# Linear attention and channel mixing on one core: batch 0's loads first on the two hardware queues, weights and batch 1 in a forced order, and a hand-set order for batch 0's attention

## The chip, the cores and the metric

The kernel runs on one core of one Trainium2 chip. The metric is the device time of one execution in microseconds (us). A ratio is the mean time of one kernel's runs over the mean time of the other's runs of the same rounds on the same chip. It is therefore not quite the ratio of the medians that are quoted beside it. The profile comes from one execution, and its span is about 1.8 us shorter than the device time.

## The reference

There are 8 batches of 8 heads, 576 rows and 64 columns. A softmax over the columns of q, a softmax over the rows of k, and two small products give x, which then goes through a channel-mixing block (512 to 1024 to 512).

```python
q_s = softmax(q, axis=-1)              # over 64 columns
k_s = softmax(k, axis=2)               # over 576 rows
kv  = einsum('bhsd,bhse->bhde', k_s, v)
x   = einsum('bhsd,bhde->bhse', q_s, kv)   # -> (8, 576, 512)
x_prev = x shifted down by one row, zeros first
xk = mu_k * x + (1 - mu_k) * x_prev
xr = mu_r * x + (1 - mu_r) * x_prev
out = sigmoid(xr @ w_r) * (maximum(xk @ w_k, 0) ** 2 @ w_v)
```

## The kernel before

The work of a batch comes in two halves of four heads each. A half loads q, k and v (576 KB each, as float32). ScalarE takes exponentials of q and k and casts v. VectorE normalises q. TensorE forms `kvp`, transposes q into `qtp`, and forms `xp`. ScalarE copies `qt` and `xb` out, and VectorE mixes neighbouring rows into `xk` and `xr`. The channel mixing then runs in units of 512, 384 and 256 rows per pair of batches. It projects `xk` with `wk_bf` (`kfp`), takes relu on ScalarE (`rel`) and the square on VectorE (`k2`), and then does two more products (`rp`, `vp`). The attention of later batches is interleaved with the units. In these traces an engine that waits for data starts no later instruction of its own (ScalarE stands for 4.03 us below while the relus behind it have their data).

```python
ldpool = ctx.enter_context(tc.tile_pool(name="ldpool", bufs=3))
...
for m, src in enumerate((moe_mu_k, moe_mu_r)):       # four small transfers, first on ScalarE's queue
    for g in range(2):
        ...
        nc.scalar.dma_start(out=mu_sb[...], in_=ap)
emit_load(0, 0, (nc.sync, nc.scalar, nc.sync))       # q, k, v of the first half
first = emit_load(0, 1, (nc.scalar, nc.sync, nc.scalar))[0]
...
def emit_weights(gate):     # wk and wr in four transfers each of whole rows, wv in two,
    ...                     # all on GpSimd's queue, all gated on `first` (q of the second half)

def unit(pair, c0, n):
    for fc in range(FT):
        kfp = psum.tile([128, 512], F32, tag="mm", bufs=4, name="kfp")
        for ct in range(CT):                         # ct 0, 1: first half; ct 2, 3: second half
            nc.tensor.matmul(kfp[:, 0:n], lhsT=wk_bf[:, ct, fc * 128:(fc + 1) * 128],
                             rhs=xk[:, ct, c0:c0 + n], start=(ct == 0), stop=(ct == CT - 1))
        rel = mpool.tile([128, 512], BF16, tag="rel", bufs=3, name="rel")
        nc.scalar.activation(out=rel[:, 0:n], in_=kfp[:, 0:n], func=ACT.Relu, scale=HALF_ROOT)
        nc.vector.tensor_tensor(out=k2[:, fc, 0:n], in0=rel[:, 0:n], in1=rel[:, 0:n], op=ALU.mult)
        yield n
    ...

emit_weights(first)
a0 = attention(0, 0); next(a0)
a1 = attention(0, 1); next(a1)
emit_mu()                                            # transpose mu on TensorE, copy on VectorE
emit_load(1, 0, (nc.gpsimd,) * 3)                    # batch 1
emit_load(1, 1, (nc.gpsimd,) * 3)
```

The order of these statements is not the order on the engines. A scheduler reorders instructions of the program by its own estimate of when they will be ready, except on engines where the kernel asks for its own order.

The softmax here doesn't subtract the row's maximum and nothing guards it: scores larger than these inputs give would overflow.

## Time and profile before

The median of three runs was 223.57 us (223.4 to 224.09).

| | before |
|---|---|
| TensorE busy, share of the span | 191.7 us, 86% |
| TensorE idle before 33 us | 33 − 12.00 = 21.0 us |
| ScalarE busy from 33 to 58 us | 25.00 of 25 us |
| first kv product starts | 13.75 us |
| first projection on the second half's xk | 29.55 us |
| first relu | 31.95 us |

The page's first part gives each engine's busy time, its share of the span, and the number of instructions.

```profile
span 221.9 us, 3634 instructions
PE 191.7 (86%) x1313; PEld 101.5 (46%) x1313; DVE 166.2 (75%) x367; ACT 147.7 (67%) x229; POOL 37.3 (17%) x58
```

The windows view of the kernel before comes next. Its columns are the window and its length, then the busy us (and instructions) of PE, PEld, DVE, ACT and POOL, then the granted clock of TensorE, the share of the DMA engines, and GB/s.

```profile
0.00:33.00 33.00, 12.00 (x81) 6.72 (x81) 18.08 (x43) 15.57 (x17) 13.57 (x25) 1.00 0.95 258
33.00:48.00 15.00, 13.80 (x107) 7.10 (x107) 13.70 (x30) 15.00 (x21) 5.66 (x8) 1.00 1.02 381
48.00:58.00 10.00, 9.00 (x63) 4.74 (x63) 9.78 (x20) 10.00 (x15) 4.94 (x8) 1.00 1.03 402
```

The first row shows the head: 21 us of TensorE's idle time lie there. ScalarE is busy for every microsecond from 33 to 58 us, while TensorE loses 1.2 us and then 1.0 us.

The timeline of the kernel before follows, with start, length, engine, line, operation, and in brackets the idle time before and what ended it.

```profile
4.95 1.28 ACT L155 ACT_TABLE_LOAD   x1 [4.95 <-DMA raw<-in_q_dram]
11.49 1.16 ACT L155 ACTIVATE eqk<-raw 128x1152 bf16<-128x1152 f32 x1 [4.08 <-DMA raw<-in_k_dram]
13.26 2.40 POOL L118 DMA_DIRECT2D wk_bf<-in_moe_w_k_dram  x4 [10.96 <-DMA raw<-in_q_dram]
13.75 1.16 PE L175 MATMUL kvp<-vv_100,eqk 64*128 64x129 bf16 x18 [7.12 <-ACT vv_100 L159]
...
29.55 1.89 PE L223 MATMUL kfp<-xk,wk_bf 128*128 128x512 bf16 x8 [1.91 <-DVE xk L212]
30.88 1.16 ACT L155 ACTIVATE eqk<-raw 128x1152 bf16<-128x1152 f32 x1 [4.03 <-DMA raw<-in_k_dram]
31.95 0.58 ACT L227 ACTIVATE rel<-kfp 128x512 bf16<-128x512 f32 x1
```

The first half's k lands at 11.4 us and holds up ScalarE. The weights are issued only at 13.26 us. ScalarE then stands 4.03 us in front of k of batch 1, and the relus come behind it, in order, although projection sums already exist. The chain of the work that ended last says the same:

```profile
2.67 10.29 DMA raw<-in_q_dram
14.45 5.93 DMA wk_bf<-in_moe_w_k_dram
20.66 10.20 DMA raw<-in_k_dram
30.88 1.16 ACT eqk L155
```

Up to 31 us, the kernel before is one chain of transfers: the gate for the weights, the weights, then batch 1.

### The profile page before, as it was taken

What the parts mean: (1) busy time and instruction counts of PE and PEld (TensorE: products, weight loads), DVE (VectorE), ACT (ScalarE), POOL (GpSimd) and SP (SyncE); (2) the same over time, 40 slices, a digit from 0 to 9 for tenths busy, and PEclk for the clock granted to TensorE, in tenths of its full rate; (3) what the DMA queues carried; (4) which work ended last, traced back from release to release, by engine and by line L of the source; (5) the groups of instructions that cost most, each with busy time, mean ns of one, the idle gap of its engine ahead of it and who ended that gap; (6) DMA issues with size and microseconds to landing.
All of it is one profiled execution on the core that took longest, in us unless ns stands there. A gap on an engine that the chain in (4) does not pass through costs nothing.

```text
span 221.9 us, 3634 instructions
## 1 busy us (share of the span) xinstructions
PE 191.7 (86%) x1313; PEld 101.5 (46%) x1313; DVE 166.2 (75%) x367; ACT 147.7 (67%) x229; POOL 37.3 (17%) x58
## 2 busy tenths in 40 slices
PE   0045748999999999999999999999999999999990
PEld 0033214444547554445547454446465544454640
DVE  1539758999999898889798998888777757482431
ACT  1396449999976969685939697849736392653440
POOL 2066713253330030330030300000000000000000
PEclk9999999999999999999999999999999999999999
DMA  6979999999999274789075290242131401330413
GB/s 231 385 196 163 205 373 391 390 368 402 414 361 340 108 245 168 228 276 319 14 239 222 42 360 16 50 96 47 35 88 24 95 3 30 76 83 21 108 29 83
DMA packets 15691, 40.61 MB, mean 183 GB/s; under 512 B 2105, under 2 KB 3641, under 8 KB 15673
## 3 DMA queue, kind: packets, MB, share of 16 engines
q0 software_dynamic: 8256, 27.40, 38.4%
q1 hardware_dynamic: 6576, 11.21, 17.2%
q10 hardware_dynamic: 840, 1.77, 2.1%
q8 instruction: 10, 0.16, 0.3%
q14 instruction: 9, 0.07, 0.1%
HBM read 33.56 MB, written 9.44 MB: 194 GB/s over the span
## 4 chain that ended last, share of the span: by engine, by line
PE 57%; DVE 15%; DMA 12%; ACT 10%; issue 2%; ACTq 1%; POOL 1%; DVEq 0%
PE vp L242 23%; PE kfp L223 15%; PE rp L235 11%; DMA raw<-in_q_dram 5%; DMA raw<-in_k_dram 5%; PE xp L195 3%; ACT rel L227 3%; ACT eqk L155 3%; ACT qt L190 3%; DMA wk_bf<-in_moe_w_k_dram 3%; PE kvp L175 3%; DVE rsum L163 2%; DVE xk L212 2%; DVE xm L210 2%; PE qtp L189 2%
## 5 line engine op out<-in xcount | busy, mean ns | idle before, releaser
L223 PE MATMUL kfp<-xk,wk_bf 128*128 128x384 bf16 (+2 forms) x384 | 71.1, 329 | 4.0 <-DVE xk L212 2.3
L227 ACT ACTIVATE rel<-kfp 128x512 bf16<-128x512 f32 (+2 forms) x96 | 45.8, 517 | 20.7 <-PE kfp L223 19.4
L223 PEld LDWEIGHTS <-wk_bf 128*128 128x128 bf16 x384 | 35.8, 98 | 28.8 <-issue 6.8
L155 ACT ACTIVATE eqk<-raw 128x1152 bf16<-128x1152 f32 x32 | 37.9, 1200 | 12.1 <-DMA raw<-in_k_dram 8.1
L245 DVE SCALAR_TENSOR_TENSOR ot<-th,vp 128x512 f32<-128x512 f32 x36 | 24.6, 683 | 17.5 <-PE vp L242 12.7
L238 ACT ACTIVATE th<-rp 128x512 f32<-128x512 f32 x36 | 22.9, 635 | 21.9 <-PE rp L235 20.9
L235 PE MATMUL rp<-wr_bf,xr 128*128 128x512 bf16 x144 | 37.0, 379 | 0.0
L163 DVE TENSOR_REDUCE rsum<-eqk 128x18 f32<-128x1152 bf16 x16 | 21.6, 1349 | 6.5 <-ACT eqk L155 6.4
L74 POOL DMA_DIRECT2D raw<-in_q_dram x14 | 10.2, 731 | 73.2 <-ACT vv_108 L159 31.8
L167 DVE TENSOR_TENSOR qs<-eqk,rrec 128x1152 bf16<-128x1152 bf16 x16 | 21.7, 1356 | 0.8
L210 DVE TENSOR_SCALAR xm<-xd,mu 128x576 bf16<-128x576 bf16 x64 | 21.4, 377 | 0.4
L190 ACT COPY qt<-qtp 128x1152 bf16<-128x1152 bf16 x16 | 18.2, 1137 | 4.3 <-PE qtp L189 4.1
L235 PEld LDWEIGHTS <-xr 128*128 128x128 bf16 x144 | 13.2, 98 | 13.9
L195 PE MATMUL xp<-qt,w 128*128 128x512 bf16 x64 | 13.8, 303 | 5.9 <-ACT qt L190 5.6
L175 PEld LDWEIGHTS <-eqk 64*128 64x128 bf16 x288 | 9.6, 100 | 14.4 <-issue 8.2
L195 PEld LDWEIGHTS <-w 128*128 128x128 bf16 x64 | 6.3, 101 | 14.1 <-issue 7.2
L189 PE MATMUL qtp<-ident,qs 128*128 128x128 bf16 x144 | 11.6, 231 | 0.0
L189 PEld LDWEIGHTS <-qs 128*128 128x128 bf16 x144 | 9.9, 103 | 2.6 <-issue 0.4
L175 PE MATMUL kvp<-vv_100,eqk 64*128 64x129 bf16 x108 | 4.7, 233 | 7.3 <-ACT vv_100 L159 7.3
L74 POOL DMA_DIRECT2D raw<-in_v_dram x14 | 10.1, 723 | 2.3 <-DMA wv_bf<-in_moe_w_v_dram 1.8
L74 POOL DMA_DIRECT2D raw<-in_k_dram x14 | 10.1, 721 | 2.3 <-DMA wv_bf<-in_moe_w_v_dram 1.4
L182 DVE SCALAR_TENSOR_TENSOR w<-kvp,rz,mask 128x128 bf16<-128x128 f32 x32 | 9.7, 339 | 0.4
(81 smaller groups left out, 234.4 us busy)
## 6 DMA issues: line engine op xcount, KB each, us to landing
out_dram<-ot SPq DMA_DIRECT2D x72, 128.0 KB, 2.4
raw<-in_q_dram POOLq DMA_DIRECT2D x14, 576.0 KB, 7.1
raw<-in_k_dram POOLq DMA_DIRECT2D x14, 576.0 KB, 8.0
raw<-in_v_dram POOLq DMA_DIRECT2D x14, 576.0 KB, 9.2
wk_bf<-in_moe_w_k_dram POOLq DMA_DIRECT2D x4, 256.0 KB, 5.4
wv_bf<-in_moe_w_v_dram POOLq DMA_DIRECT2D x2, 512.0 KB, 9.7
raw<-in_q_dram SPq DMA_DIRECT2D x1, 576.0 KB, 3.8
raw<-in_v_dram SPq DMA_DIRECT2D x1, 576.0 KB, 4.8
```

Source lines behind the costliest of these rows:

```text
L74: ld.append(queues[i].dma_start(out=t[:, i, :, :], in_=ap))
L155: nc.scalar.activation(out=eqk[:, i, :, :, :], in_=t[:, i, :, :].rearrange("p u (j d) -> p j u d", d=D), func=ACT.Exp)
L163: nc.vector.reduce_sum(out=rsum[:], in_=eq, axis=AX.X)
L189: nc.tensor.transpose(out=qtp[:, j, :], in_=qs[:, j, :], identity=ident[:])
L190: nc.scalar.copy(out=qt[:], in_=qtp[:, 0:J, :])
L195: nc.tensor.matmul(xp[:, 64 * c:64 * e], lhsT=w[:, hf, :], rhs=qt[:, c:e, 64 * hf:64 * hf + 64], start=True, stop=True)
L210: nc.vector.tensor_scalar(out=xm[:, hf, :], in0=xd[:, hf, :], scalar1=mu[:, c:c + 1], scalar2=None, op0=ALU.mult)
L223: nc.tensor.matmul(kfp[:, 0:n], lhsT=wk_bf[:, ct, fc * 128:(fc + 1) * 128], rhs=xk[:, ct, c0:c0 + n], start=(ct == 0), stop=(ct == CT - 1))
L227: nc.scalar.activation(out=rel[:, 0:n], in_=kfp[:, 0:n], func=ACT.Relu, scale=HALF_ROOT)
L235: nc.tensor.matmul(rp[:], lhsT=xr[:, ct, c0 + 128 * m:c0 + 128 * m + 128], rhs=wr_bf[:, ct, :], start=(ct == 0), stop=(ct == CT - 1))
L242: nc.tensor.matmul(vp[:], lhsT=k2[:, ft, 128 * m:128 * m + 128], rhs=wv_bf[:, ft, :], start=(ft == 0), stop=(ft == FT - 1))
L245: nc.vector.scalar_tensor_tensor(out=ot[:], in0=th[:], scalar=1.0, in1=vp[:], op0=ALU.add, op1=ALU.mult)
```

## The change

The intent was to shorten the head. Batch 0 is to arrive on two hardware queues with q and k first. The weights start as soon as batch 0's first half is in. Batch 1 follows in a forced order, and batch 0's attention runs in an order set by hand on TensorE, VectorE and ScalarE. The diff, cut to its core:

```diff
-    ldpool = ctx.enter_context(tc.tile_pool(name="ldpool", bufs=3))
+    ldpool = ctx.enter_context(tc.tile_pool(name="ldpool", bufs=4))
+    ctx.enter_context(tc.manual_schedule(engines={mybir.EngineType.Pool}))
     (a half is now heads 0,1,4,5 or 2,3,6,7 instead of four neighbours)
+    first = emit_load(0, 0, (nc.sync, nc.scalar, nc.sync))
     for m, src in enumerate((moe_mu_k, moe_mu_r)):
-        for g in range(2):
-            nc.scalar.dma_start(out=mu_sb[...], in_=ap)
-    emit_load(0, 0, (nc.sync, nc.scalar, nc.sync))
-    first = emit_load(0, 1, (nc.scalar, nc.sync, nc.scalar))[0]
+        nc.sync.dma_start(out=mu_sb[4 * m:4 * m + 4, :]..., in_=ap)
+    emit_load(0, 1, (nc.scalar, nc.sync, nc.scalar))
+    warm = const.tile([1, 1], F32, name="warm")
+    nc.vector.memset(warm[:], 0.0)
+    nc.scalar.activation(out=warm[:], in_=warm[:], func=ACT.Exp)
...
+        for h in range(2):                      # wk in column halves: 2 KB runs of the source
+            for u in range(2):
+                ld = part(wk_bf, moe_w_k, F, u, 512 * h, 512 * h + 512)
+                (the first one gated on v of the first half)
+        for u in range(2):
+            part(wr_bf, moe_w_r, C, u, 0, C)
...
-    def unit(pair: int, c0: int, n: int):
+    def unit(pair: int, c0: int, n: int, step: int = 1):
     (with step 4: four kfp tiles get ct 0, 1 first, and then all four get ct 2, 3)
...
+    emit_weights(first[2]); emit_load(1, 0); emit_load(1, 1)
+    with tc.manual_schedule(engines={PE, DVE, Activation}):
+        emit_mu()
+        a0 = Attention(0, 0); a1 = Attention(0, 1)
+        a0.exp(0); a0.exp(1); a0.norm_q(); a0.cast_v(nc.scalar.copy); a1.exp(0)
+        a0.kv("mm"); a0.transpose_q(); a0.copy_qt(); a0.weights()
+        a1.exp(1); a1.norm_q(); a0.x(0); a0.x(1); a1.cast_v(nc.scalar.copy)
+        a1.kv("mm"); a1.transpose_q(); a1.copy_qt(); a0.diff(); a0.mix(0)
+        a1.weights(); a1.x(0); a1.x(1); a1.diff(); a1.mix(0); a0.mix(1); a1.mix(1)
...
-            for c in unit(pair, c0, n):
+            for c in unit(pair, c0, n, 4 if pair == 0 and c0 == 0 else 1):
```

## The prediction

> **What bounds it now.** The page puts TensorE at 191.7 us busy of a 221.9 us span. The windows view places its idle time: 21 us before 33 us, only some 4 us between 33 and 208 us, and about 5 us at the tail. The body is bound by TensorE; only the head can give.
>
> **Head, from the timeline and the waits.** q of the first half batch lands at 4.95 us; ScalarE then loads its table (1.28 us, exposed). k of that half lands only at 11.4 us, behind four mu transfers on its queue and beside batch 1's q (issued at 1.47 us). The v cast, and with it the first kv product, waits to 13.7 us. The weights wait for the second half's q (13.26 us). Batch 1's q is handled in the middle of batch 0's chain (1.2 us ScalarE, 3.0 us VectorE). The second half's xk releases the projection at 29.55 us; ScalarE, in order, stands 4.03 us in front of batch 1's k (lands 30.88 us) before the first relu at 31.95 us.
>
> **What changes, with my estimate.** Rates come from the page: 385 GB/s once running; weights move about 5.2 MB of f32 in some 15 us.
> - Batch 0 alone on two queues: q and k at about 5.2 us, v about 8.3 us, the second half about 12 us. First kv product about 9.5 us instead of 13.7.
> - Table load hidden: 1.3 us on ScalarE, not on the final chain.
> - Against it: the mu transpose and copy now come first in the forced order, and mu is queued behind q and v, so the first row sum may wait until 8.5 us (1.4 us lost).
> - Summing measured durations along the hand-set order (exp 1.16, cast 1.14, qt 1.1, row sum plus reciprocal plus multiply 3.0, w 0.8, mix 1.5 us), the second half's xk is ready at about 24 to 25.6 us, 4 to 5.5 us sooner.
> - Weights, gated on v, start at about 8.5 us and leave no gap in the transfers. All engines share the transfers (the Trainium skill, "DMA: Bandwidth & Descriptors", section "Issuing engines are not separate DMA queues"), so bytes decide: batch 1 then comes whole at about 35 us, only 1 to 3 us sooner than before, its q later than before. This caps the gain: either ScalarE again stands before batch 1's exponentials ahead of relus, or TensorE idles 2 to 3 us before the second unit.
> - TensorE work, tail and steady state: unchanged. The interleaved start exists already (eight first matmuls ran before 29.55 us).
>
> **Result.** The head gives 4 to 6 us if the relus run ahead of batch 1, 1 to 3 us if not; I hold the first the likelier. Predicted 218.3 us, 80% range 214.5 to 221.8. Chances: faster by over 2% 0.58, within 2% 0.38, slower by over 2% 0.04.
>
> **Right or wrong in the profile after.** TensorE busy 190 to 192 us. First kv product near 9.5 to 10 us. Weight issues begin near 8.5 us. First projection matmuls on channels 2 and 3 at 24 to 26 us. Second unit's (128x384) steady matmuls at 47 to 52 us instead of 54.8. TensorE idle before 33 us falls by about 5 us; later it rises by at most 3.
>
> **What would make it wrong.** ScalarE or VectorE, ordered ahead of the data, stalled by batch 1's load; wk column halves (2 KB runs instead of 4 KB) moving slower; two queues not giving k by 6 us; VectorE, nearly full from 33 to 80 us, unable to give batch 1 earlier, so the head's gain returns as idle TensorE.

## The result, and the profile after

The kernel after took 221.38 us in the median of four runs (220.91 to 221.84). The kernel before took 223.66 us in the same rounds (223.4 to 224.09). The ratio is 0.9896 (0.9869 to 0.9922), a gain of 1.0% where I had forecast 2.4%. Executions over 1.5% slower than the fastest of the same kernel are left out of the means.

```profile
span 219.7 us, 3641 instructions
PE 193.5 (88%) x1313; PEld 101.6 (46%) x1313; DVE 166.3 (76%) x384; ACT 147.7 (67%) x230; POOL 35.8 (16%) x56
```

The same windows of the kernel after:

```profile
0.00:33.00 33.00, 14.96 (x88) 7.89 (x89) 17.34 (x45) 16.57 (x21) 13.86 (x25) 0.95 1.03 272
33.00:48.00 15.00, 14.15 (x112) 7.13 (x110) 14.88 (x34) 15.00 (x22) 5.68 (x9) 1.00 1.03 394
48.00:58.00 10.00, 8.98 (x74) 4.83 (x73) 9.99 (x21) 10.00 (x15) 3.67 (x6) 1.00 1.04 406
```

TensorE did 3.0 us more of busy time before 33 us, though with a clock that read 0.95 on average. ScalarE did only 1.0 us more before 33 us, and again it is full from 33 to 58 us.

The timeline of the kernel after, with the lines that answer to those shown of before:

```profile
5.97 2.22 ACT L154 ACTIVATE eqk<-raw 128x1152 bf16<-128x1152 f32 x2 [2.17 <-DMA raw<-in_q_dram]
9.36 1.15 ACT L160 CAST vv_103<-raw 128x1152 bf16<-128x1152 f32 x1 [1.17 <-DMA raw<-in_v_dram]
9.64 2.62 POOL L113 DMA_DIRECT2D wk_bf<-in_moe_w_k_dram  x4 [8.33 <-DMA raw<-in_v_dram]
10.16 1.34 DVE L166 TENSOR_REDUCE rsum<-eqk 128x18 f32<-128x1152 bf16 x1
10.56 1.16 PE L184 MATMUL kvp<-vv_103,eqk 64*128 64x129 bf16 x18 [0.53 <-ACT vv_103 L160]
...
27.82 6.73 PE L270 MATMUL kfp<-xk,wk_bf 128*128 128x512 bf16 x23 [2.92 <-DVE xk L232]
28.95 1.16 ACT L154 ACTIVATE eqk<-raw 128x1152 bf16<-128x1152 f32 x1 [3.68 <-DMA raw<-in_q_dram]
30.02 1.07 ACT L276 ACTIVATE rel<-kfp 128x512 bf16<-128x512 f32 x2
```

The first kv product came 3.2 us sooner (10.56 instead of 13.75 us), and the weights 3.6 us sooner (9.64 instead of 13.26 us). The projection on the second half's xk came only 1.7 us sooner (27.82 instead of 29.55 us) and the first relu 1.9 us. ScalarE still stands in front of batch 1, now in front of its q, for 3.68 us.

The chain of the kernel after, at its start and where it turns:

```profile
2.20 7.45 DMA mu_sb<-in_moe_mu_r_dram
...
21.01 2.56 PE kfp L270 x6
...
27.82 6.73 PE kfp L270 x23
...
36.04 0.64 ACT rel L276
36.67 1.01 ACT qt L207
37.68 0.50 ACT rel L276
38.18 0.49 ACT th L287
```

It starts with a transfer of 2 KB of mu, holds six projection matmuls that stand ahead of the second half's xp products, then 23 matmuls in 6.73 us. From 36.04 to 58.01 us nearly every piece of it is ScalarE. In the kernel before, most of the chain in the same stretch is VectorE, for example:

```profile
36.13 1.36 DVE rsum L163
38.06 1.27 DVE qs L167
41.88 0.75 DVE xk L212
44.17 1.26 DVE rsum L163
```

Summed from 33 to 58 us, ScalarE has 5.0 us of the chain before and 21.8 us after, and VectorE 15.3 and 0 us. Both engines are nearly full there, so the chain runs over one or the other by small differences: in bufs3, below, whose time is nearly that of the kernel after, it is 10.1 and 9.5 us.

As a measure of progress I compare the ends of the VectorE instructions that write the output tiles (36 in each kernel, in order). After minus before is −2.50 us at tile 1, −2.08 at tile 4, −1.88 at tile 8 (which ends at 77.99 us before), and −1.53 at tile 10 (91.95 us). It then stays between −1.53 and −1.70 us to the last tile. (Between tiles 1 and 10 the difference jumps, to −1.16 at tile 2 and −2.53 at tile 5, so single tiles say little.) Everything but the tail was therefore decided before about 92 us. A further 0.6 us of the spans' difference of 2.2 us comes after the last tile.

### The profile page after: what moved, and what is told of

Same layout as the page of the kernel before. It is cut to its first block, busy times and chain, and to the rows that moved or that the text cites. A ratio compares the mean times of both kernels' runs of the same rounds, so it can differ in the third digit from the quotient of the medians.

```text
span 219.7 us, 3641 instructions
## 1 busy us (share of the span) xinstructions
PE 193.5 (88%) x1313; PEld 101.6 (46%) x1313; DVE 166.3 (76%) x384; ACT 147.7 (67%) x230; POOL 35.8 (16%) x56
## 2 busy tenths in 40 slices
DMA packets 16171, 40.62 MB, mean 185 GB/s; under 512 B 2072, under 2 KB 4632, under 8 KB 16152
## 4 chain that ended last, share of the span: by engine, by line
PE 60%; ACT 19%; DVE 13%; DMA 3%; issue 2%; SPq 1%; DVEq 0%; ACTq 0%
PE vp L291 22%; PE kfp L270 19%; PE rp L284 11%; ACT eqk L154 5%; ACT qt L207 4%; ACT rel L276 4%; DMA mu_sb<-in_moe_mu_r_dram 3%; PE kvp L184 3%; PE qtp L202 3%; PE xp L212 2%; DVE rsum L166 2%; DVE xk L232 2%; DVE qs L170 2%; ACT xb_105 L215 2%; ACT xb_109 L215 1%
## 5 line engine op out<-in xcount | busy, mean ns | idle before, releaser
L270 PE MATMUL kfp<-xk,wk_bf 128*128 128x384 bf16 (+2 forms) x384 | 72.6, 335 | 4.3 <-DVE xk L232 3.7
L270 PEld LDWEIGHTS <-wk_bf 128*128 128x128 bf16 x384 | 36.3, 99 | 30.3 <-issue 8.5
```

## The experiments

Eighteen kernels ran. Each ratio is against the kernel before in the same rounds. Some of the expectations name engines by the short names that the profile uses (PE is TensorE, DVE VectorE, ACT ScalarE, POOL GpSimd).

### Which part of the change gave the gain?

**loads_only** keeps the loads, queues and GpSimd order of the kernel after, but leaves batch 0's attention to the scheduler as before:

```diff
-    with tc.manual_schedule(engines={PE, DVE, Activation}):
-        ... the hand-set order ...
+    a0 = attention(0, 0); next(a0)
+    a1 = attention(0, 1); next(a1)
+    emit_mu()
+    for gen in (a0, a1): drain(gen)
-            for c in unit(pair, c0, n, 4 if pair == 0 and c0 == 0 else 1):
+            for c in unit(pair, c0, n):
```

> The changed kernel's loads (queues, weight pieces, gate on v, four raw buffers, forced GpSimd order, early table load), but batch 0's attention emitted as before, in the scheduler's own order, and no interleaved start. If the loads make the gain (theory A: batch 1's arrival and the full ScalarE and VectorE after it set the pace): about 221.4 us, as the change. If the hand-set order makes it (theory H: the chain of batch 0 sets the pace): about 223.5 us. If both give part: 222 to 223 us.

**order_only** is the reverse: the loads, weights and three buffers of the kernel before, with the hand-set order and step 4.

> The kernel before's loads, queues, weight pieces and three raw buffers, with the hand-set order of batch 0's attention and the interleaved start. Theory H: about 221.5 to 222 us. Theory A: 223 to 224 us, as before, since batch 1 arrives as before.

Loads_only took 221.27 us, ratio 0.9877 (0.9854 to 0.9899), which is no worse than the whole change. Order_only took 224.67 us, ratio 1.0036 (1.001 to 1.0063), so a little slower than before. The gain came from the loads; the hand-set order added nothing that these runs show. In order_only the second half's xk was ready 0.4 us sooner than before (29.06 us), but ScalarE took k and v of batch 1 first, at 30.90 and 32.41 us, and the first relu came at 33.46 us, 1.5 us later than before.

**mu_moved** is the kernel before with one edit: the four mu transfers go to the other hardware queue, behind the first half's loads.

```diff
+    emit_load(0, 0, (nc.sync, nc.scalar, nc.sync))
     ...
-            nc.scalar.dma_start(out=mu_sb[...], in_=ap)
+            nc.sync.dma_start(out=mu_sb[...], in_=ap)
-    emit_load(0, 0, (nc.sync, nc.scalar, nc.sync))
```

> The kernel before with one thing changed: the four mu transfers go out on SyncE's queue behind the first half batch's loads, so that the first half's k is first on ScalarE's queue. (The scheduler then also puts batch 1's q behind the weights by itself, as in pool_forced, which alone was 0.6% slower.) If the queue place of k is what delays batch 0 in the kernel before: k lands by 7 us instead of 11.4, the first kv product starts at about 10.5 us, the weights are gated earlier too, and the time is about that of loads_only, 221 to 222 us (ratio 0.986 to 0.993). If the gain needs the other load edits (gate on v, wk pieces, four buffers): 223 to 225 us.

It took 222.4 us, ratio 0.9938 (0.9906 to 0.9969), which is about six tenths of the whole change's gain by the middle values. The exponentials of q and k began at 5.76 us and the first kv product at 10.89 us, nearly as in the kernel after. Its six runs fall into two groups (220.99 to 221.79 and 223.0 to 223.27 us), which I can't explain. The scheduler also moved batch 1's q behind the weights in this kernel, so the edit is not as pure as its diff; pool_forced, next, has that move alone.

**pool_forced** is the kernel before with only the forced GpSimd order added.

> The kernel before with one line more: the GpSimd order is the program's order, so that batch 1's q no longer goes out at 1.5 us but after the weights. Nothing else of the change. If the head start of batch 1's q is what delays batch 0 before (k lands at 11.4 us), about half or more of the change's gain comes from this line: 221.5 to 222.5 us, first kv product at 11 to 12 us. If the other load edits matter (queues, mu off ScalarE's queue, gate on v), 223 to 223.6 us.

It took 225.27 us, ratio 1.0063 (1.0026 to 1.01). The second half's xk was ready at 28.59 us, 0.9 us sooner than before (29.50 us), and yet the kernel was slower. Its first kv product came at 12.71 us, 1.0 us sooner than before, where mu_moved had it 2.9 us sooner; so batch 1's early q was only a part of what delayed batch 0, and the place of mu on the queue the larger part. ScalarE waited 4.86 us for batch 1's q, took it at 30.66 us and its k at 32.16 us, and the first relu came at 33.23 us. **bufs3**, the kernel after with three load buffers, tested the fourth buffer.

> The changed kernel with three raw buffers instead of four; the order on ScalarE is the same. If the fourth buffer has a part in the gain (it lets batch 2's first half be fetched before batch 1's v is cast): 222 to 223 us. If not: 221 to 221.6 us.

It took 221.59 us, ratio 0.9915 (0.9896 to 0.9935), against 0.9896 for the kernel after. The intervals overlap, so the fourth buffer has no part that these runs can show.

### Was it the half clock of TensorE?

The windows of one microsecond show the granted clock of the kernel after at the start of its first unit:

```profile
27.00:28.00 1.00, 0.18 (x1) 0.10 (x1) 0.99 (x3) 0.00 (x0) 0.31 (x1) 0.84 1.00 407
28.00:29.00 1.00, 1.00 (x3) 0.29 (x2) 0.96 (x3) 0.05 (x1) 0.40 (x1) 0.50 1.06 424
31.00:32.00 1.00, 1.00 (x5) 0.39 (x4) 1.00 (x3) 1.00 (x2) 0.68 (x1) 0.95 1.01 383
```

The clock fell to 0.50 after 2.92 us of idle TensorE and stayed there for 3.4 us (from 27.68 to 31.10 us in the trace's clock record). Before, TensorE idled 1.91 us at the same place, and the clock read 1.00. The Trainium skill, "TensorE: Matmul & The Clock Gate", section "What's actually happening", describes such a thing: half the clock after an idle window of some 3.4 us, full clock again after as much activity, with windows that run free of the kernel. The trace agrees on the window's length, but the window before the fall (24.27 to 27.68 us) was not idle throughout: TensorE was busy for 0.63 us of it. Over nineteen traces, each of the 28 recorded windows of 3.41 us at full clock in which TensorE was busy for 0.395 of the time or less is followed by the half clock, and none of the 1041 with 0.422 or more is. The kernel before just escaped, with 0.44 in the window from 26.83 us. (The clock column also reads 1.00 where a trace holds no clock record yet. In the kernel before the record begins at 26.83 us, and 18 kv matmuls take 1.16 us at 13.75 us, against 0.70 us at 33.62 us.) So here was a rival explanation for the missing gain. **filler** adds ten matmuls on data of the first half, into a scratch tile, between the two channel halves of the first group, to keep TensorE busy:

```diff
+                if step > 1 and f0 == 0 and cts[0] == 2:
+                    idle = psum.tile([128, 1024], F32, tag="att", bufs=2, name="idle")
+                    for _ in range(10):
+                        nc.tensor.matmul(idle[:, 0:512], lhsT=wk_bf[:, 0, 0:128],
+                                         rhs=xk[:, 0, c0:c0 + n], start=True, stop=True)
```

> The changed kernel with ten extra matmuls of 512 columns into a scratch tile, put on TensorE between the two halves of the first projection group, where the change has TensorE idle for 2.92 us and its granted clock then falls to 0.50 from 27.8 to 31.0 us. Theory C (the idle gap costs the clock, and the slow matmuls cost time): no half clock after the gap, the 23 projection matmuls take about 5 us instead of 6.73, and the time falls by 1 to 1.5 us, to about 220 us (ratio 0.982 to 0.985). Rival: the clock falls too but ScalarE, which has batch 1's q exponential and the relus in order, sets the pace, and the time stays at 221.4 us (ratio 0.989).

It took 221.65 us, ratio 0.9883 (0.9852 to 0.9914). The clock stayed at 1.00, as it was meant to. Its timeline, in the lines of the first unit, shows what the clock was worth:

```profile
27.94 1.89 PE L275 MATMUL kfp<-xk,wk_bf 128*128 128x512 bf16 x8 [0.72 <-DVE xk L232]
29.49 1.16 ACT L154 ACTIVATE eqk<-raw 128x1152 bf16<-128x1152 f32 x1 [4.35 <-DMA raw<-in_q_dram]
...
31.19 3.70 PE L275 MATMUL kfp<-xk,wk_bf 128*128 128x512 bf16 x15 [1.36 <-ACT rel L281]
```

Eight matmuls took 1.89 us at full clock, and then TensorE waited 1.36 us for a relu. The half clock was real, and its removal gained nothing here, where TensorE then stood waiting for relus. Theory C falls for this kernel. (The profile caught filler's slowest execution, 222.56 us.)

That the half clock costs nothing in general is not shown. The record has the mean granted clock of every execution, and in kernels with a faster head, which come next, a lower clock and a longer time go together. Mu_kfp took 220.0 to 221.18 us in its four executions at 0.996 or more, and 221.81 and 221.91 us in the two at 0.992. Mu_kfp_rel4 took 220.4 and 220.54 us at 1.0, and 221.08 to 222.03 us in its three other fast ones at 0.988 and 0.989. That is about 1 us, but only an association, since idle TensorE time also lowers the clock. Loads_only shows none.

### The head made as short as I had predicted it

Two things had made the head of the kernel after later than my sum. The row sum stood behind the mu copy, which waited for mu until 9.8 us. And six half-speed projection matmuls, from 21.0 to 23.6 us, stood ahead of the second half's xp products. **mu_pool** sends mu on GpSimd's queue, first of all:

```diff
-        nc.sync.dma_start(out=mu_sb[4 * m:4 * m + 4, :]..., in_=ap)
+        nc.gpsimd.dma_start(out=mu_sb[4 * m:4 * m + 4, :]..., in_=ap)
```

> The changed kernel with the two mu transfers on the GpSimd queue at the very start. The first row sum then starts at about 7.2 us instead of 10.16 us, and the second half's xk is ready 1 to 1.6 us before the 27.8 us of the change. Theory H: the time falls by as much, to about 220 us (ratio to before 0.983). Theory A: the time stays at 221 to 221.5 us (ratio 0.988 to 0.991), because ScalarE still waits for batch 1's q and is full from then on.

**kfp_after_x** puts the first projection group after the second half's xp products in the forced order:

```diff
         a1.x(1)
+        u0 = unit(0, 0, 512, 4)
+        early = [next(u0) for _ in range(1)]
```

> The changed kernel with the first projection group held behind the second half's x products on TensorE (in the change six half-clock projection matmuls, 2.6 us, stand between them and the qt copy, which is done at 22.2 us while the x products start at 23.36). Theory H: x products about 1.1 us sooner, second half's xk ready at about 26.7 us; and since the eight projection matmuls now fill the gap before it, no half clock at 27 to 31 us either; together 1.5 to 2.5 us faster than the change, 219 to 220 us. If ScalarE's wait for batch 1's q (28.9 us) sets the pace: no more than 0.5 us faster.

**mu_kfp** does both.

> Both: mu on the GpSimd queue at the start, and the first projection group behind the second half's x products. Theory H: the gains add up, second half's xk at about 25.2 us, and the time 2.5 to 3.5 us below the change, 218 to 219 us, which is what was predicted for the change. If batch 1's arrival sets the pace: no better than the better of the two alone.

| | xk of the second half ready | first relus | time, median | ratio |
|---|---|---|---|---|
| after (own rounds) | 27.8 | 30.02 | 221.38 | 0.9896 (0.9869 to 0.9922) |
| mu_pool | 26.3 | 27.41, 29.31, 30.84 | 220.78 | 0.9863 (0.9833 to 0.9893) |
| kfp_after_x | 27.1 | 29.80 | 223.56 | 0.9974 (0.994 to 1.0008) |
| mu_kfp | 25.1 | 26.17, 29.59 | 220.84 | 0.9863 (0.9828 to 0.9898) |

The first row sum of mu_pool began at 8.18 us, near the 8.5 us of my prediction. In mu_kfp the second half's xk was ready at 25.1 us, inside the 24 to 25.6 us that I had predicted for the change. Yet the time fell by only about half a microsecond against the kernel after, with intervals that overlap. The timeline of mu_kfp shows where those 2.6 us went:

```profile
26.17 0.60 ACT L277 ACTIVATE rel<-kfp 128x512 bf16<-128x512 f32 x1 [3.64 <-PE kfp L271]
28.52 1.16 ACT L155 ACTIVATE eqk<-raw 128x1152 bf16<-128x1152 f32 x1 [1.75 <-DMA raw<-in_q_dram]
29.59 0.58 ACT L277 ACTIVATE rel<-kfp 128x512 bf16<-128x512 f32 x1
30.22 1.02 PE L271 MATMUL kfp<-xk,wk_bf 128*128 128x512 bf16 x4 [1.93 <-ACT rel L277]
```

One relu ran early. Behind it ScalarE, in order, waited 1.75 us for batch 1's q, and the second relu came after that exponential at 29.59 us. TensorE, with its four buffers full, idled 1.93 us. Kfp_after_x had xk sooner than the kernel after and was still slower by its ratio. Its profile caught its fastest run (222.22 us at a clock of 0.998; the five others, at 0.985 to 0.992, took 223.36 to 224.42 us), so I don't explain the ratio from that trace. The clock is a likely part of it.

**mu_filler** put the filler into mu_pool, in case the clock mattered once mu was early. It took 221.93 us, ratio 0.9929 (0.9906 to 0.9952), so no help and rather a loss. But its trace still shows the half clock, from 32.63 to 36.04 us, so the filler did not do what it was for and the question stays unanswered.

> mu_pool with the ten extra matmuls of filler: xk at about 26.3 us, no half clock after the idle gap. If the half clock costs time once the relus run (in mu_pool one relu is ahead of batch 1's q): 219.5 to 220.2 us, 0.5 to 1 us under mu_pool. If not: 220.5 to 221 us.

### Relus first, and batch 1 sooner

If ScalarE's order is the obstacle, relus should go ahead of batch 1. **mu_kfp_rel4** is mu_kfp with four relus forced ahead of batch 1's exponentials:

```diff
+        u0 = unit(0, 0, 512, 4)
+        early = [next(u0) for _ in range(4)]
+        next(att)               # batch 1's first exponentials, after the four relus
```

> The kernel mu_kfp with ScalarE's order forced: the first four relus of the first unit before batch 1's first exponentials (in all kernels so far at least one relu stands behind the exponential of batch 1's q, whose data lands at 28.2 to 29.5 us, so a faster head could not be used). Theory S (ScalarE, in order, stands before batch 1's data with relus behind it): the faster head of mu_kfp (xk at 25.1 us) now counts; fourth relu over by about 28.5 us instead of 33.1, TensorE no longer idle at 29 to 30 us, and the time 2 to 4 us under the change, 217.5 to 219.5 us (ratio 0.971 to 0.980). Rival B (the arrival of the whole of batch 1 and the full ScalarE and VectorE after 33 us set the pace whatever the relus do): about as mu_kfp, 220.5 to 221 us.

It took 221.52 us, ratio 0.9872 (0.9843 to 0.9902). Forcing the relus ahead gained nothing alone.

**b1_before_wv** brings the other side forward: batch 1's first half is loaded before wv.

> The changed kernel with batch 1's first half loaded ahead of wv. Batch 1's q lands about 5 us sooner than the 28.9 us of the change (2.1 MB less ahead of it at about 0.39 MB per us). Theory A: 2 to 4 us faster than the change, 218 to 219.5 us. Theory H: no difference, 221 to 221.5 us, or slower if wv now comes late.

It took 222.9 us, ratio 0.9954 (0.9925 to 0.9983), which is slower than the kernel after. Batch 1's exponentials now ran at 25.05 us, in the middle of batch 0's chain. Its row sum on VectorE began at 26.79 us, ahead of the last xk (28.05 us), which was ready at 28.8 us.

**light_dma** does not load the second half of wv and uses the first half twice, so its result is wrong. It only tests what batch 1 would be worth with 1 MB less ahead of it.

```diff
-        for h in range(2):
+        for h in range(1):
-                                 rhs=wv_bf[:, ft, :], ...
+                                 rhs=wv_bf[:, ft % (FT // 2), :], ...
```

> Wrong result on purpose: the changed kernel without the transfer of the second half of wv (1.05 MB of f32 read), its matmuls reading the first half twice; the same work on every engine. Batch 1's transfers then land about 2.7 us sooner (q at about 26.3 us, v of the second half at about 35.3 instead of 38.0). If batch 1's arrival sets the pace, in the form S or B: 1.5 to 2.7 us faster than the change, 218.7 to 220 us. If the head's own chain does: 221.4 us.

**rel4_light_dma** joins it with mu_kfp_rel4, and is wrong too.

> Wrong result on purpose: mu_kfp_rel4 without the second half of wv. If S alone holds, this is about as mu_kfp_rel4 (the relus no longer stand behind batch 1). If batch 1's arrival still counts after the relus are freed (B): another 1 to 2.5 us faster than mu_kfp_rel4.

Light_dma took 221.17 us, ratio 0.9873 (0.9848 to 0.9897), with batch 1's q used at 26.12 us instead of 28.95. Rel4_light_dma took 219.65 us, ratio 0.9804 (0.9784 to 0.9825). Batch 1 sooner alone moved little, relus and head alone moved little, and both together moved 1.7 to 1.9 us by the medians. This fits two limits that end at nearly the same time, each hiding what the other is worth. The clock is a rival that these runs do not separate: against the two executions of mu_kfp_rel4 at full clock (220.4 and 220.54 us) the step to rel4_light_dma, which ran at 0.994 to 1.0, is only 0.8 us.

The correct form of the pair is **rel4_b1**: mu_kfp_rel4, with batch 1's first half loaded before wv.

> A correct kernel that loosens both waits at once: mu_kfp_rel4 (faster head, four relus ahead of batch 1's exponentials) with batch 1's first half loaded ahead of wv, so that ScalarE's exponentials at about 28 us find their data (q lands at 23.7, v at 26.6 us instead of 31.9). Theory P (head and batch 1's arrival bind in parallel: each loosened alone gave nothing, light_dma 221.2 and mu_kfp_rel4 221.5 us, both together 219.65 us): 219 to 220.3 us. If only the whole of batch 1 (its last v, 38 us) counts: 221 to 222 us, as mu_kfp_rel4.

It took 220.15 us, ratio 0.9844 (0.982 to 0.9868).

### The column halves of wk

**wk_full** is the kernel after with wk in two transfers of whole 4 KB rows instead of four with 2 KB runs.

```diff
-        for h in range(2):
-            for u in range(2):
-                ld = part(wk_bf, moe_w_k, F, u, 512 * h, 512 * h + 512)
+        for u in range(2):
+            ld = part(wk_bf, moe_w_k, F, u, 0, F)
```

> The changed kernel with wk in two transfers of whole rows (4 KB runs of f32, as in the kernel before) instead of four column halves (2 KB runs); ScalarE's order is the same. In the change the weights start 3.6 us sooner than before, yet batch 1's last v lands 1.2 us later (38.0 against 36.8 us). If the short runs make wk slow: batch 1's q lands 0.7 to 1.5 us sooner than 28.95 us, and the time falls by 0.5 to 1.2 us. If not: q lands within 0.4 us of 28.95 us and the time stays at 221.4 us.

It took 220.68 us, ratio 0.9863 (0.984 to 0.9885). The page counts 4632 packets under 2 KB in the kernel after, 3641 before and 3576 here. ScalarE's first exponential of batch 1 began at 28.02 us; in the kernel after it was 28.95 us:

```profile
28.02 1.16 ACT L153 ACTIVATE eqk<-raw 128x1152 bf16<-128x1152 f32 x1 [3.88 <-DMA raw<-in_q_dram]
```

That is 0.93 us sooner at equal bytes, although the first weight issue was 0.16 us later (9.80 us). The tiles from the tenth on came 2.49 us before those of the kernel before, instead of 1.53. The size is not certain, because the landing varies: in five other kernels with the kernel after's loads ScalarE began on batch 1's q at 28.73 to 29.49 us, and in mu_pool at 28.24 us. The wk transfer itself is the better measure. From its first issue to its last landing it took 9.02 us here and 8.45 us in rel4_b1_wk, and 9.40 to 10.59 us in the thirteen kernels with column halves whose profile is in the fast state. So whole rows are faster, and their worth in time, about 0.7 us, is only likely, since the ratios' intervals overlap.

**rel4_b1_wk** puts whole rows into rel4_b1. It is correct.

> The best correct kernel so far (rel4_b1, 220.15 us) with wk in whole rows. If the short runs are slow: about 0.5 to 1 us under rel4_b1, 219.2 to 219.7 us. If not: 220 to 220.3 us.

It took 219.5 us (219.34 to 219.54 in five runs), ratio 0.9805 (0.9786 to 0.9823). This is the best correct kernel, 1.95% under the kernel before. Its windows:

```profile
0.00:33.00 33.00, 16.06 (x117) 8.87 (x118) 20.21 (x50) 19.06 (x24) 14.65 (x26) 1.00 1.03 289
33.00:48.00 15.00, 14.18 (x98) 7.08 (x96) 14.67 (x32) 15.00 (x20) 6.39 (x9) 1.00 1.03 395
48.00:58.00 10.00, 9.29 (x72) 4.94 (x71) 9.97 (x25) 9.96 (x17) 3.61 (x6) 1.00 1.04 407
```

ScalarE did 19.06 us of work before 33 us, against 16.57 in the kernel after and 15.57 before.

### Is VectorE the pace of the first units?

VectorE is nearly full as well from 33 us on (14.88 of 15 us in the kernel after). **light_dve** takes the row sums of batches 1 and 2 over 16 of the 64 columns; its result is wrong.

```diff
-            nc.vector.reduce_sum(out=rsum[:], in_=eq, axis=AX.X)
+            nc.vector.reduce_sum(out=rsum[:], axis=AX.X,
+                                 in_=eq[:, :, 0:16] if self.b in (1, 2) else eq)
```

> Wrong result on purpose: the changed kernel with the row sums of batches 1 and 2 over 16 of 64 columns, so that VectorE has about 4 us less work between 29 and 60 us, where it is 99% busy; orders elsewhere hardly changed. If VectorE's full stretch sets the pace: 1.5 to 4 us faster, 217.5 to 220 us. If arrival and ScalarE's order do: within 0.7 us of the change.

It took 221.09 us, ratio 0.9866 (0.9845 to 0.9888), against 0.9896 for the kernel after. VectorE fell to 13.60 us between 33 and 48 us, ScalarE was still busy 14.95 of 15 us there, and the time hardly moved. So VectorE's load is worth about 0.3 us by the medians, and the intervals overlap. By chance the clock also read 1.00 throughout in the head of the profiled execution (220.98 us), and the executions at 0.989 to 0.991 took 220.84 to 221.23 us, which agrees with filler that the half clock is worth little in this order.

## Why the prediction was wrong, point by point

The time itself, 221.38 us, lies just inside the predicted range (214.5 to 221.8 us), but the gain was less than half of the forecast.

**"The head gives 4 to 6 us if the relus run ahead of batch 1 ... I hold the first the likelier."** This is the step that failed, in three terms.

1. *The second half's xk at 24 to 25.6 us.* It came at 27.8 us. v landed at 9.36 instead of 8.3 us. The mu wait that I had put at 8.5 us lasted until 9.8 us, with the row sum at 10.16 us; mu_pool took this away and won 1.5 us of xk. The six projection matmuls ahead of the xp products were not in my sum; with them moved as well, mu_kfp reached 25.1 us. So this term of the sum was mis-sized by 2.2 us at least, and its two causes are shown.
2. *"Batch 1 then comes whole at about 35 us, only 1 to 3 us sooner."* It came 1.2 us later than before: its last load landed at 38.0 us (issued at 22.81 us, 15.2 us on the way), against 36.8 us before. The bytes did decide, as the Trainium skill, "DMA: Bandwidth & Descriptors", section "Issuing engines are not separate DMA queues", let me assume: all queues share the same engines. But I took the rate for unchanged. The column halves of wk delayed batch 1 by about 1 us (q by 0.93 us and the last load from 36.99 to 38.0 us against wk_full), a risk that I had named and not costed. That makes up the loss against before, but not the 1 to 3 us that I had expected to win; those stay unexplained. (These are single executions; in five other kernels with the same loads the last load landed at 37.15 to 38.53 us.) Before, moreover, one load of batch 1 (its q, issued at 1.47 us) had been moved ahead of the weights, and after the change all of batch 1 stands behind them.
3. *The relus ahead of batch 1.* They did not run ahead. ScalarE waited 3.68 us for batch 1's q and the relus came behind it, which is the branch for which I had written 1 to 3 us. The wait ended 1.9 us sooner than before (28.95 instead of 30.88 us), and the first relu came 1.9 us sooner. The measured gain, 2.3 us, lies in this branch, but in part by luck: I had based 1 to 3 us on batch 1 coming whole that much sooner, and it came later. The second unit's steady matmuls, for which I had said 47 to 52 us, started at 53.54 us (before: 54.76).

The condition in that step was not enough either. Mu_kfp_rel4 forces the relus ahead of batch 1 on the head of mu_kfp, and still took 221.52 us (220.4 and 220.54 us at full clock), against 224.22 us for the kernel before in its rounds: a gain of 2.7 us by the medians, and not of 4 to 6. Only with batch 1 brought sooner as well did a correct kernel reach the forecast gain: rel4_b1_wk, with xk at 24.9 us, took 219.5 us against 223.82 us for the kernel before in its rounds, 4.3 us less.

**"The body is bound by TensorE; only the head can give."** This holds from 58 us on (before, TensorE is busy for 148.22 of the 150 us from 58 to 208 us), but not from 33 to 58 us. There ScalarE has no idle time in the kernel before, nor in the kernel after, and VectorE little (1.5 and 0.1 us), while TensorE idles 2.2 and 1.9 us. This is a likely reason why even a head of the predicted length (mu_kfp) gave only half a microsecond more: what counts at the end of the head is then perhaps not when TensorE gets its xk, but how much of its work ScalarE has done by then. ScalarE did 1.0 us more before 33 us in the kernel after. Over nineteen profiles (before, after and seventeen experiments), ScalarE's busy time up to 58 us and the span have a correlation of −0.92, with a slope of −1.2 us of span per us. Examples are pool_forced (39.4 us busy, 223.8 us span), before (40.57, 221.9), after (41.57, 219.7), mu_kfp (42.59, 218.7) and rel4_b1_wk (44.02, 217.6). Light_dma (43.52, 218.9) and b1_before_wv (42.29, 220.6) lie about 1 us above that line, and light_dve (41.45, 219.2) 1.3 us below it. In b1_before_wv batch 1's work had gone ahead of batch 0's; in light_dma the projection was hardly sooner than in the kernel after (27.59 against 27.82 us). So ScalarE's amount of work is not all; which work comes first counts too.

This reading of ScalarE is an association found after the runs, and a weak one: any kernel that is ahead by 58 us has also done more on every engine. VectorE's busy time up to 58 us correlates with the span almost as well (−0.89, without light_dve), and the chain of the kernel before runs mostly over VectorE there. In the runs, VectorE's load (light_dve), TensorE's clock in the order of the kernel after (filler), the buffers (bufs3) and the head alone (mu_kfp) were each worth some tenths of a microsecond at most by the medians, and head and batch 1 together were worth more. No run lightened ScalarE itself between 33 and 58 us, so that it is the pace of this stretch is not shown.

**The hand-set order.** I gave it a share of the gain, as the way to xk at 24 to 25.6 us. It gave nothing (loads_only 0.9877, order_only 1.0036). The scheduler's own order with the new loads had xk ready at 27.54 us, 0.2 us sooner than the hand-set order.

**What was right, or nearly.** q landed by 5.97 us and k within the first exponential's time, on two queues. The first kv product came at 10.56 us (predicted 9.5 to 10) and the weights were issued at 9.64 us (predicted 8.5). The table load moved off the way of batch 0: the Trainium skill, "ScalarE: Activation LUTs", section "What ACT_TABLE_LOAD costs", gives 1283 ns for it, and both traces show 1.28 us, exposed at 4.95 us before and hidden at 2.31 us after. I had said that it would not count on the final chain. TensorE's busy time (193.5 us) came out just above the predicted 190 to 192: it rose by 1.8 us, of which the 23 matmuls at half clock account for about 1.3 us (an estimate: 6.73 us, where eight take 1.89 us in filler). TensorE's idle time before 33 us fell by 3.0 us (21.0 to 18.0), where I had said 5.

**What stays open.** The 0.6 us of the gain after the last output tile has no explanation; loads_only has it whole, order_only 0.2 us of it. Why the lead of the kernel after shrinks from 2.5 to 1.5 us between 65 and 92 us was not isolated. The spread of 1 us and more between executions goes with the clock in mu_kfp, mu_kfp_rel4, kfp_after_x and mu_filler, but not in mu_moved, where it stays unexplained; it limits what differences of half a microsecond can say.

## What to carry to other kernels

Before a head is shortened, read which engine is full in the stretch just after it: time saved at the entrance can be lost there, and a second limit that ends at nearly the same time can hide what either is worth alone, so test both together. Compare executions at the same granted clock before reading differences of 1 us. An instruction that waits for late data on an in-order engine blocks ready work behind it; place it after the ready work, or bring its data sooner. Put the first large transfer ahead of the small ones on its queue, and keep the source runs long where transfers fill the time.

## What the Trainium skill lacked or had wrong

- **"DMA: Bandwidth & Descriptors", section "Specifications":** it gives 512 bytes as the least transfer for line rate. Here 2 KB runs of a float32 source, cast to bf16 on the way, were slower than 4 KB runs: wk's 2.1 MB took 9.40 to 10.59 us from issue to landing in thirteen kernels, against 9.02 and 8.45 us in the two with 4 KB runs. "Perfetto Trace Analysis", section "DMA Optimizations", which advises going from 2 KB to 4 KB, agrees with this measurement.
- **"TensorE: Matmul & The Clock Gate", section "What's actually happening":** it speaks of an idle window of about 3.4 us, and not of how idle. Here the half clock came after every window of 3.41 us in which TensorE was busy for 0.395 of the time or less (28 windows in nineteen traces), and after none with 0.422 or more (1041 windows).
- **No page that I looked at** warns that removing the half clock may be worth nothing where TensorE is not what the others wait for: filler removed it, and TensorE then waited 1.36 us for ScalarE at an unchanged time.
